# Running the middle row transform of a spectral gate's backward pass in two turns: a pair's back matmuls placed after the next pair's forward matmuls, and tiny edge copies moved to VectorE

## The chip, the cores and the metric

The kernel runs on one core of a Trainium2 chip, as one launch. The metric is the device time of that launch in microseconds (us), the median over several runs.

## The reference

The kernel computes a gated mix of two branches and all gradients of it. `x` has 2048 rows of 1024 values.

```python
def _A_ref(x, w_r, w_i):                       # spectral branch
    X = rfft2(x) * (w_r + 1j * w_i)            # w: 2048 x 513
    return irfft2(X, s=(2048, 1024))
def _B_ref(x, w1, b1, w2, b2):                 # dense branch, 1024 -> 3584 -> 1024
    r = relu(x @ w1 + b1)
    return (r * r) @ w2 + b2
g = sigmoid((x * gate_w).sum(-1))
out = g * _A_ref(A_x, ...) + (1 - g) * _B_ref(A_x, ...)
...
_out, _vjp = jax.vjp(_f, A_x, A_w_r, A_w_i, B_w1, B_b1, B_w2, B_b2, gate_w)
return (_out, *_vjp(grad_out))
```

So there are nine outputs: the mix, and the gradients of `x`, of both parts of the spectral weight, of the dense branch's four parameters, and of the gate's weight. Inputs and outputs are bfloat16.

## The kernel before

The two-dimensional transform of `x` and that of the output's gradient are made together, as matmuls with constant matrices in 16-bit floats. The 2048-point transform along the rows is split into 32 times 64 points. The dense branch's large matmuls keep TensorE busy meanwhile. In order of time:

1. `mlp_in`: the hidden layer and its gradient (`ph`, `pd`), with the first stage of the transform between its matmuls: columns and the 32-point part of the rows. The result goes to `z_scr` in memory.
2. `mlp_grads`: the gradients of the dense weights. Each of 112 turns is a group of 16 accumulating matmuls into one `pw` bank, 128x512 (L778 for the second weight, L794 for the first), emptied by a ScalarE copy `wo` (L782, L799). There are two `pw` banks, so a group can start only when the copy of the group two before it is done. Between these turns runs `spectra()`: first `fft_mid`, the middle of the row transform, which is what the change is about, then part of `fft_out`, the last stage of the transform.
3. `mlp_out`: the dense branch's output (`acc`, L866), with the rest of `fft_out` between.
4. `GradOfX.products`: the gradient of `x` (`xX`, `xV`, `xZ`, L966).

`fft_mid` handles the 32 columns of the 32x64 split in 16 mirrored pairs `m`. For each pair, before the change:

- `inputs` loads `z` (four transfers) and the rows `w` of the spectral weight (four more), for the next pair.
- `transform`: for pairs other than the first, VectorE makes `pm`, the sum and the difference of the two columns (L356, L357). Twice (n = 0, 1) two matmuls write `px` (L364), and two ScalarE copies, on 64 partitions each, put it into `x` in another order (L366). They take 2450 ns each.
- GpSimd writes the pair's edge values into `x` (L455), and it negates a row of `w` (L373).
- `products`: VectorE multiplies `x` by `w` into `t1_`, `t2_` (L377, L379) and joins them into `y` (L384, L385, twice each).
- `back`: for n = 1, 0 two matmuls write `pv` (L394). For n = 1 ScalarE copies it to `vc` (L399); for n = 0 VectorE makes `pc` from it and `vc` (L401, L402). GpSimd copies edge values of `y` into `ye` (L408 to L414), two tiny matmuls make `si` of it (L417), two tiny VectorE copies put it into `pc` (L421 to L425), and four stores from GpSimd's queue write `pc` to `y_scr` (L428).
- `grads_of_w`: VectorE makes `gs` from `x` (L434 to L438), ScalarE scales it to `gw` (L440), VectorE halves its edge values (L441), and GpSimd's queue stores it (L444).

`px` and `pv` take turns in two buffers of PSUM, two banks each (tag `ps2`). `x`, `z`, `w` and `pc` have two buffers, `pm`, `y`, `vc`, `gs` and `gw` one.

The order of the work is set by generators. `fft_mid` yields seven times for a pair. `spread` hands out `spectra()` between the turns of the gradients at a constant rate:

```python
spec, grads = spectra(), mlp_grads()
next(grads), next(grads)
todo = 1 + 7 * (R1 // 2) + 2 * NT
for _ in spread(grads, spec, todo / (2.0 * FG * FGC * NH - 2)):
    pass
```

That is 145 yields over 110 turns, about 1.32 a turn. [...]A scheduler at build time sets the order in a queue from this program order and its own idea of the durations, so a row may stand a little earlier or later than the program has it. `fft_mid` of before:

```python
for m in range(NM):
    ...
    for x in transform(m, z):
        yield
    G.tensor_copy(out=x[:, :, :, 0::H], in_=ex[:, m])
    for y in products(x, w):
        yield
    yield from back(m, y)
    grads_of_w(m, x)
    yield
```

Of the kernel before, what the change touches and what calls it, by code (L numbers as in the profile page):

```python
# [10 lines left out]
P = 128  # L11
BF16 = mybir.dt.bfloat16
FP16 = mybir.dt.float16
FP32 = mybir.dt.float32
ALU = mybir.AluOpType
ACT = mybir.ActivationFunctionType

FDT = FP16
# [117 lines left out]
def kernel(  # L136
# [22 lines left out]
    nc = tc.nc  # L159
# [6 lines left out]
    g = Geo(S, D, F)  # L166
    S2, DC, FC = g.S2, g.DC, g.FC
    R1, R2 = g.R1, g.R2
    NT = S // P
# [132 lines left out]
    def fft_mid():  # L302
# [9 lines left out]
        def inputs(m):  # L312
            z = fb.tile([P, 2, 2, H], FDT, name="z", tag="z", bufs=2)
            for n, c in enumerate((m, R1 // 2 + m)):
                for x in range(2):
                    ld(out=z[lanes[x], n], in_=z_scr[:][c, :, x ^ n if m else x])
            w = fb.tile([P, 3, LW], BF16, name="w", tag="w", bufs=2)
            for c_, src_w in enumerate((A_w_r, A_w_i)):
                for n, k in enumerate(pair_of(m, R1)):
                    ld(out=w[lanes[n], c_, 0:W1], in_=every(src_w, k))  # L320
            return z, w

        def edges():

            ed = fb.tile([P, NM, 2, 4], FDT, name="ed", tag="ed")
            low = fb.tile([P, NM, 4], FDT, name="low", tag="low")
            mid = fb.tile([P, 4], FDT, name="mid", tag="mid")
            col = z_scr[:].rearrange("c r x t l -> r c (x t) l")[:, :, :, 0]
            for e in range(4):
                ld(out=ed[lanes[0], :, 0, e], in_=col[:, 0:NM, e])  # L330
                ld(out=low[lanes[1], :, e], in_=col[:, NM:, e])
            ld(out=mid[lanes[0]], in_=col[:, NM])
            nc.vector.tensor_copy(out=ed[lanes[0], :, 1, :], in_=ed[lanes[0], :, 0, :])
            nc.vector.tensor_copy(out=ed[lanes[0], 0, 1, :], in_=mid[lanes[0]])
            for n in range(2):
                a, b = slice(2 * n, 2 * n + 2), slice(2 - 2 * n, 4 - 2 * n)
                nc.vector.tensor_copy(out=ed[lanes[1], :, n, a], in_=low[lanes[1], :, a])
                nc.vector.tensor_scalar(out=ed[lanes[1], :, n, b], in0=low[lanes[1], :, b], scalar1=-1.0, scalar2=None, op0=ALU.mult)
            nc.vector.memset(ed[lanes[1], 0], 0.0)
            sp = tps.tile([P, NM, 2, 4], FP32, name="sp", tag="tr", bufs=2)  # L340
            for m in range(NM):
                for n in range(2):
                    mm(sp[:, m, n], lhsT=am[:, m, n, :], rhs=ed[:, m, n, :], start=True, stop=True, skip_group_check=True)
            ex = fb.tile([P, NM, 2, 2, 2], FDT, name="ex", tag="ex")
            for n in range(2):
                for c in range(2):
                    nc.vector.tensor_copy(
                        out=ex[lanes[n], :, c], in_=sp[lanes[c], :, n, :].rearrange("p m (e t) -> p m t e", e=2)
                    )
            return ex  # L350

        def transform(m, z):

            if m:
                pm = fb.tile([P, 2, 2, H], FDT, name="pm", tag="pm")
                V(out=pm[:, 0], in0=z[:, 0], in1=z[:, 1], op=ALU.add)  # L356
                V(out=pm[:, 1], in0=z[:, 0], in1=z[:, 1], op=ALU.subtract)  # L357
            else:
                pm = z
            x = fb.tile([P, 2, 2, LW], FDT, name="x", tag="x", bufs=2)  # L360
            for n in range(2):
                px = fps.tile([P, 2, H], FP32, name="px", tag="ps2", bufs=2)
                for T in range(2):
                    mm(px[:, T, :], lhsT=am[:, m, n, :], rhs=pm[:, n, T, :], start=True, stop=True)  # L364
                for c in range(2):
                    nc.scalar.copy(  # L366
                        out=x[lanes[n], c, :, 0:H].rearrange("p t (i g) -> p t g i", g=4),
                        in_=px[lanes[c]].rearrange("p t (g i) -> p t g i", g=4),
                    )
                yield x  # L370

        def products(x, w):
            G.tensor_scalar(out=w[:, 2, 0:W1], in0=w[:, 1, 0:W1], scalar1=-1.0, scalar2=None, op0=ALU.mult)  # L373
            t1_ = fb.tile([P, 2, 2, LW], FDT, name="t1", tag="t1")
            t2_ = fb.tile([P, 2, 2, LW], FDT, name="t2", tag="t2")
            xw = lambda t: t[:].rearrange("p c t l -> p (c t) l")[:, :, 0:W1]
            V(out=xw(t1_), in0=xw(x), in1=w[:, 0:1, 0:W1].to_broadcast([P, 4, W1]), op=ALU.mult)  # L377
            wi = w[:, 1:3, 0:W1].rearrange("p (o t) l -> p o t l", o=1).to_broadcast([P, 2, 2, W1])
            V(out=t2_[:, :, :, 0:W1], in0=x[:, :, :, 0:W1], in1=wi, op=ALU.mult)  # L379
            yield  # L380
            y = fb.tile([P, 2, 2, LW], FDT, name="y", tag="y")
            for n in (1, 0):
                L = lanes[n]
                V(out=y[lanes[0], n, :, 0:W1], in0=t1_[L, 0, :, 0:W1], in1=t2_[L, 1, :, 0:W1], op=ALU.subtract)  # L384
                V(out=y[lanes[1], n, :, 0:W1], in0=t1_[L, 1, :, 0:W1], in1=t2_[L, 0, :, 0:W1], op=ALU.add)  # L385
            yield y

        def back(m, y):
            pc = fb.tile([P, 2, 2, H], FDT, name="pc", tag="pc", bufs=2)
            pv = {}  # L390
            for n in (1, 0):
                pv[n] = fps.tile([P, 2, H], FP32, name="pv", tag="ps2", bufs=2)
                for T in range(2):
                    mm(pv[n][:, T, :], lhsT=bm[:, m, n, :], rhs=y[:, n, T, 0:H], start=True, stop=True)  # L394
                if m == 0:
                    nc.scalar.copy(out=pc[:, n], in_=pv[n][:])
                elif n == 1:
                    vc = fb.tile([P, 2, H], FP32, name="vc", tag="vc")
                    nc.scalar.copy(out=vc[:], in_=pv[1][:])  # L399
                else:  # L400
                    V(out=pc[:, 0], in0=pv[0][:], in1=vc[:], op=ALU.add)  # L401
                    V(out=pc[:, 1], in0=pv[0][:], in1=vc[:], op=ALU.subtract)  # L402
                yield

            ye = fb.tile([P, 2, 2, 2], FDT, name="ye", tag="ye", bufs=2)
            yl = y[:, :, :, H]
            if m:
                G.tensor_copy(out=ye[:, :, 0, :], in_=yl)  # L408
                G.tensor_copy(out=ye[:, 1, 1, :], in_=yl[:, 1])
                G.tensor_scalar(out=ye[:, 0, 1, :], in0=yl[:, 0], scalar1=-1.0, scalar2=None, op0=ALU.mult)  # L410
            else:
                G.memset(ye[:], 0.0)
                for n in range(2):
                    G.tensor_copy(out=ye[:, n, n, :], in_=yl[:, n])  # L414
            sp = tps.tile([P, 2, 2], FP32, name="si", tag="tr", bufs=2)
            for n in range(2):
                mm(  # L417
                    sp[:].rearrange("p a t -> p (a t)"), lhsT=bm[:, m, n, :], rhs=ye[:, n].rearrange("p a t -> p (a t)"),
                    start=(n == 0), stop=(n == 1), skip_group_check=True,
                )  # L420
            nc.vector.tensor_copy(out=pc[lanes[1], 0, :, 0], in_=sp[lanes[0], 0, :])  # L421
            if m:
                nc.vector.tensor_copy(out=pc[lanes[0], 1, :, 0], in_=sp[lanes[1], 1, :])
            else:
                nc.vector.tensor_copy(out=pc[lanes[1], 1, :, 0], in_=sp[lanes[0], 1, :])  # L425
            for n, c in enumerate((m, R1 // 2 + m)):
                for h in range(2):
                    st(out=y_scr[:][c, :, h ^ n if m else h], in_=pc[lanes[h], n])  # L428
# [16 lines left out]

        nxt = inputs(0)
        ex = edges()
        yield
        for m in range(NM):
            z, w = nxt  # L450
            if m + 1 < NM:
                nxt = inputs(m + 1)
            for x in transform(m, z):
                yield
            G.tensor_copy(out=x[:, :, :, 0::H], in_=ex[:, m])  # L455
            for y in products(x, w):
                yield
            yield from back(m, y)
            grads_of_w(m, x)
            yield  # L460
        fbs.close()

    def fft_out():
# [680 lines left out]
    for k in range(NT // 4):  # L1144
        i = 4 * k
# [38 lines left out]
    n = 0  # L1184
# [25 lines left out]

    spec, grads = spectra(), mlp_grads()
    next(grads), next(grads)
    todo = 1 + 7 * (R1 // 2) + 2 * NT
    for _ in spread(grads, spec, todo / (2.0 * FG * FGC * NH - 2)):
        pass
    tps_s.close()
# [45 lines left out]
```

## The time and the profile before

| what | value |
|---|---|
| median time of 3 runs | 1378.58 us (1378.45 to 1379.13) |
| span of the profiled run | 1377.1 us |
| TensorE (PE) busy | 1283.7 us, 93% |
| VectorE (DVE) busy | 697.4 us, 51% |
| ScalarE (ACT) busy | 581.7 us, 42% |
| GpSimd (POOL) busy | 271.8 us, 20% |
| granted TensorE clock, mean | 0.968 |
| the four x copies of a pair (L366), all pairs | 156.8 us in 64 copies |
| negation of w on GpSimd (L373), all pairs | 24.5 us in 16 |
| GpSimd's tiny copies into `ye` and `x` (L408 to L414, L455) | 10.6 + 9.2 + 6.2 + 1.3 + 3.6 us |

A row of the profile names the line, the engine, what is written and read, and how often. PE is TensorE's matmul, PEld its load of the stationary operand, which lies beside the matmuls. In the view of waits a row says which instruction waited for which, for how long in total, how often, and the longest. In the timeline the number in brackets is the idle time of that engine just before, with what ended it. `mlp_grads` runs from 446 to about 984 us, and the 16 pairs of `fft_mid` from about 465 to 880 us. A busy TensorE is not TensorE at full speed: records of matmuls overlap, so its rate is read from the time between starts.

### The profile page before, as it was taken

What the parts mean: (1) busy time and instruction counts of PE and PEld (TensorE: products, weight loads), DVE (VectorE), ACT (ScalarE), POOL (GpSimd) and SP (SyncE); (2) the same over time, 40 slices, a digit from 0 to 9 for tenths busy, and PEclk for the clock granted to TensorE, in tenths of its full rate; (3) what the DMA queues carried; (4) which work ended last, traced back from release to release, by engine and by line L of the source; (5) the groups of instructions that cost most, each with busy time, mean ns of one, the idle gap of its engine ahead of it and who ended that gap; (6) DMA issues with size and microseconds to landing.
All of it is one profiled execution on the core that took longest, in us unless ns stands there. A gap on an engine that the chain in (4) does not pass through costs nothing.

```text
span 1377.1 us, 18208 instructions
## 1 busy us (share of the span) xinstructions
PE 1283.7 (93%) x6754; PEld 616.7 (45%) x6884; DVE 697.4 (51%) x1522; ACT 581.7 (42%) x793; POOL 271.8 (20%) x456
## 2 busy tenths in 40 slices
PE   9999999999999987987887889699999999999997
PEld 5655544555444433333333333355544445444443
DVE  4454424444822345434443543344577777795663
ACT  4656645666433465465556546244321112101110
POOL 0111111111111233432343442212100010000000
PEclk9999999999999998999899899899999999999999
DMA  9566445553437777766455665698598996845450
GB/s 294 164 181 189 140 139 167 176 171 111 128 110 172 183 177 184 191 178 151 101 146 136 145 136 117 162 319 226 168 245 187 226 228 177 229 130 168 141 150 31
DMA packets 326004, 233.27 MB, mean 169 GB/s; under 512 B 195052, under 2 KB 279178, under 8 KB 325658
## 3 DMA queue, kind: packets, MB, share of 16 engines
q1 hardware_dynamic: 290864, 141.19, 42.8%
q0 software_dynamic: 26144, 82.47, 18.0%
q10 hardware_dynamic: 8906, 8.43, 2.1%
q8 instruction: 54, 0.88, 0.3%
q14 instruction: 36, 0.29, 0.1%
HBM read 106.19 MB, written 81.81 MB: 137 GB/s over the span
## 4 chain that ended last, share of the span: by engine, by line
PE 51%; DVE 5%; ACT 4%; issue 3%; POOL 1%; DMA 1%; another core or an unknown queue 0%; POOLq 0%; ACTq 0%; DVEq 0%
PE acc L866 12%; PE pw L794 12%; PE pw L778 10%; PE xX L966 7%; PE xV L966 3%; ACT x L366 3%; PE xZ L966 2%; PE pv L394 1%; PE pki L493 1%; PE pui L294 1%; DVE t L379 1%; PE px L364 1%; DVE y L385 1%; DVE y L384 1%; DVE g L434 0%
## 5 line engine op out<-in xcount | busy, mean ns | idle before, releaser
L778 PE MATMUL pw<-dbn,grp 128*128 128x512 bf16 x876 | 214.8, 400 | 13.5 <-ACT wo L782 12.0
L637 PE MATMUL ph<-xT,w1g 128*128 128x512 bf16 x864 | 217.0, 379 | 2.7 <-DMA w1g<-in_B_w_dram 1.2
L794 PE MATMUL pw<-grp,res 128*128 128x512 bf16 x873 | 209.7, 394 | 7.8 <-ACT wo L799 6.5
L647 PE MATMUL pd<-dbT,w2T 128*128 128x512 bf16 x877 | 209.8, 379 | 1.6 <-DVE dhT L651 0.4
L866 PE MATMUL acc<-w,hblk 128*128 128x512 bf16 x873 | 196.4, 379 | 1.2
L651 DVE SCALAR_TENSOR_TENSOR dhT<-pd,rT 128x512 bf16<-128x512 f32 x112 | 77.3, 690 | 203.0 <-PE pd L647 159.8
L366 ACT CAST x<-px 64x1024 f16<-64x1024 f32 x64 | 156.8, 2450 | 3.4 <-PE px L364 2.5
L778 PEld LDWEIGHTS <-grp 128*128 128x128 bf16 x896 | 91.0, 102 | 130.0 <-issue 37.9
L794 PEld LDWEIGHTS <-res 128*128 128x128 bf16 x896 | 89.2, 101 | 115.0 <-issue 23.1
L647 PEld LDWEIGHTS <-w2T 128*128 128x128 bf16 x896 | 87.1, 98 | 103.4 <-issue 1.2
L866 PEld LDWEIGHTS <-hblk 128*128 128x128 bf16 x896 | 86.4, 98 | 98.3
L639 ACT ACTIVATE rT<-ph,b1col 128x512 bf16<-128x512 f32 x112 | 76.9, 687 | 116.1 <-PE ph L637 112.5
L637 PEld LDWEIGHTS <-w1g 128*128 128x128 bf16 x896 | 84.5, 98 | 90.5 <-DMA w1g<-in_B_w_dram 1.5
L932 ACT ACTIVATE g<-gatew_bc,dsc 128x1024 f32<-128x1024 bf16 x16 | 18.3, 1148 | 150.7 <-DVE gxo L975 124.5
L495 ACT CAST rt<-pki 128x1024 f16<-128x1024 f32 x32 | 32.5, 1017 | 97.9 <-PE pki L493 93.3
L377 DVE TENSOR_TENSOR t<-x,w 128x2052 f16<-128x2052 f16 x16 | 19.7, 1232 | 106.1 <-POOL x L455 106.0
L640 ACT ACTIVATE h2T<-rT 128x512 bf16<-128x512 bf16 x112 | 70.6, 630 | 2.5
L799 ACT CAST wo<-pw 128x512 bf16<-128x512 f32 x56 | 32.2, 585 | 92.6 <-PE pw L794 51.5
L966 PEld LDWEIGHTS <-dS 128*128 128x128 f16 x448 | 43.8, 98 | 52.9
L394 PE MATMUL pv<-y,bm 128*128 128x512 f16 x64 | 23.1, 455 | 45.9 <-DVE y L385 45.8
L782 ACT CAST wo<-pw 128x512 bf16<-128x512 f32 x56 | 31.8, 586 | 64.1 <-PE pw L778 42.2
L283 POOL DMA_DIRECT2D z_scr<-u x32 | 22.8, 714 | 171.5 <-ACT u L278 101.6
(186 smaller groups left out, 1581.9 us busy)
## 6 DMA issues: line engine op xcount, KB each, us to landing
h2T_scr<-h2T POOLq DMA_DIRECT2D x28, 512.0 KB, 4.3
dhT_scr<-dhT POOLq DMA_DIRECT2D x28, 512.0 KB, 4.7
hblk<-h2T_scr SPq DMA_DIRECT2D x8, 1792.0 KB, 9.2
hblk<-dhT_scr SPq DMA_DIRECT2D x8, 1792.0 KB, 8.8
z_scr<-u POOLq DMA_DIRECT2D x32, 256.0 KB, 3.1
z<-z_scr SPq DMA_DIRECT2D x64, 128.0 KB, 3.2
y_scr<-pc POOLq DMA_DIRECT2D x64, 128.0 KB, 2.8
r<-y_scr ACTq DMA_DIRECT2D x32, 256.0 KB, 4.3
```

The costliest lines, as they stand in the source:

```text
L366: nc.scalar.copy(out=x[lanes[n], c, :, 0:H].rearrange("p t (i g) -> p t g i", g=4), in_=px[lanes[c]].rearrange("p t (g i) -> p t g i", g=4),)
L394: mm(pv[n][:, T, :], lhsT=bm[:, m, n, :], rhs=y[:, n, T, 0:H], start=True, stop=True)
L495: nc.scalar.copy(out=rt[n][:], in_=pk[:])
L637: mm(ph[:], lhsT=w1g[:, dc, fc % 2 * P : (fc % 2 + 1) * P], rhs=xT[:, dc, ss], start=(dc == 0), stop=(dc == DC - 1))
L639: nc.scalar.activation(rT[:], ph[:], ACT.Relu, bias=b1col[:, fc : fc + 1])
L640: nc.scalar.activation(h2T, rT[:], ACT.Square)
L647: mm(pd[:], lhsT=w_[:, ec, fc % FGC * P : (fc % FGC + 1) * P], rhs=dbT[:, ec, ss], start=(ec == 0), stop=(ec == DC - 1),)
L651: return STT(out=dhT, in0=pd[:], scalar=2.0, in1=rT[:], op0=ALU.mult, op1=ALU.mult, accum_out=gb1part[:, fc, sb : sb + 1],)
L778: mm(pw[:], lhsT=cur[:, t, fb_ * P : (fb_ + 1) * P], rhs=dbn[:, t, hf * H : (hf + 1) * H], start=(t == 0), stop=(t == NT - 1),)
L794: mm(pw[:], lhsT=xr[t][:, d_ * P : (d_ + 1) * P], rhs=cur[:, t, :], start=(t == 0), stop=(t == NT - 1),)
L866: turn["PE"] = mm(acc[:], lhsT=cur[:, fc, t2 * P : (t2 + 1) * P], rhs=w2[:, fc, cs], start=(fc == 0), stop=(fc == FC - 1))
L966: mm(acc[:], lhsT=lhs[:, fc, :], rhs=rhs[:, fc, :], start=start and fc == 0, stop=fc == KH - 1, skip_group_check=True,)
```

## The change

`fft_mid` works on two pairs in turn. The forward matmuls of pair m come first; after them come the back matmuls of pair m-1, whose `y` was joined in the turn before. The purpose is that TensorE should not stand waiting for the VectorE products of the very pair whose forward matmuls it has just made. A pair's `y` and `ye` are held over to the next turn (`held`). The inputs are loaded a turn earlier, and `pm` has two buffers. A turn now has six yields, and the constant that sets the rate is changed with it.

Second, the tiny copies and the negation that GpSimd did (`w`, `ye`, the edges of `x`) run on VectorE. Nothing that is computed changes.

```diff
-        def transform(m, z):
+        def mirrored(m, z):
...
+            pm = fb.tile([P, 2, 2, H], FDT, name="pm", tag="pm", bufs=2)
...
         def products(x, w):
-            G.tensor_scalar(out=w[:, 2, 0:W1], in0=w[:, 1, 0:W1], scalar1=-1.0, scalar2=None, op0=ALU.mult)
+            nc.vector.tensor_scalar(out=w[:, 2, 0:W1], in0=w[:, 1, 0:W1], scalar1=-1.0, scalar2=None, op0=ALU.mult)
...
-                G.tensor_copy(out=ye[:, :, 0, :], in_=yl)
+                nc.vector.tensor_copy(out=ye[:, :, 0, :], in_=yl)
...
+        pm, w = mirrored(0, nxt[0]), nxt[1]
+        nxt = inputs(1)
+        held = None
         yield
-        for m in range(NM):
-            z, w = nxt
-            if m + 1 < NM:
-                nxt = inputs(m + 1)
-            for x in transform(m, z):
-                yield
-            G.tensor_copy(out=x[:, :, :, 0::H], in_=ex[:, m])
-            for y in products(x, w):
-                yield
-            yield from back(m, y)
-            grads_of_w(m, x)
-            yield
+        for m in range(NM + 1):
+            if m < NM:
+                x = fb.tile([P, 2, 2, LW], FDT, name="x", tag="x", bufs=2)
+                for n in range(2):
+                    transform(m, n, pm, x)
+                    yield
+                nc.vector.tensor_copy(out=x[:, :, :, 0::H], in_=ex[:, m])
+            if held:
+                backs = back(m - 1, *held)
+                next(backs)
+                yield
+            if m < NM:
+                ts = products(x, w)
+            if held:
+                next(backs)
+                yield
+                for _ in backs:
+                    pass
+            if m < NM:
+                held = joined(m, *ts)
+                yield
+                grads_of_w(m, x)
+                if m + 1 < NM:
+                    pm, w = mirrored(m + 1, nxt[0]), nxt[1]
+                if m + 2 < NM:
+                    nxt = inputs(m + 2)
+                yield
...
-    todo = 1 + 7 * (R1 // 2) + 2 * NT
+    todo = 1 + 6 * (R1 // 2) + 2 * NT
```

In the new code `products` ends with `t1_` and `t2_`, the join into `y` and the copies into `ye` are a function of their own (`joined`), and `back` gets both.

More of the change, by code (lines that the diff above doesn't have):

```diff
@@ L350, in edges, with transform @@
             return ex
-        def transform(m, z):
[L354 to L370, printed above, removed]
+        def mirrored(m, z):
+            if m == 0:
+                return z
+            pm = fb.tile([P, 2, 2, H], FDT, name="pm", tag="pm", bufs=2)
+            V(out=pm[:, 0], in0=z[:, 0], in1=z[:, 1], op=ALU.add)
+            V(out=pm[:, 1], in0=z[:, 0], in1=z[:, 1], op=ALU.subtract)
+            return pm
+        def transform(m, n, pm, x):
+            px = fps.tile([P, 2, H], FP32, name="px", tag="ps2", bufs=2)
+            for T in range(2):
+                mm(px[:, T, :], lhsT=am[:, m, n, :], rhs=pm[:, n, T, :], start=True, stop=True)
+            for c in range(2):
+                nc.scalar.copy(
+                    out=x[lanes[n], c, :, 0:H].rearrange("p t (i g) -> p t g i", g=4),
+                    in_=px[lanes[c]].rearrange("p t (g i) -> p t g i", g=4),
+                )
         def products(x, w):
-            G.tensor_scalar(out=w[:, 2, 0:W1], in0=w[:, 1, 0:W1], scalar1=-1.0, scalar2=None, op0=ALU.mult)
+            nc.vector.tensor_scalar(out=w[:, 2, 0:W1], in0=w[:, 1, 0:W1], scalar1=-1.0, scalar2=None, op0=ALU.mult)
             t1_ = fb.tile([P, 2, 2, LW], FDT, name="t1", tag="t1")
@@ L379, in products, with joined @@
             V(out=t2_[:, :, :, 0:W1], in0=x[:, :, :, 0:W1], in1=wi, op=ALU.mult)
-            yield
+            return t1_, t2_
+        def joined(m, t1_, t2_):
             y = fb.tile([P, 2, 2, LW], FDT, name="y", tag="y")
@@ L385, in products @@
                 V(out=y[lanes[1], n, :, 0:W1], in0=t1_[L, 1, :, 0:W1], in1=t2_[L, 0, :, 0:W1], op=ALU.add)
[L386 to L402, printed above, removed]
-                yield
             ye = fb.tile([P, 2, 2, 2], FDT, name="ye", tag="ye", bufs=2)
@@ L407, in back @@
             if m:
-                G.tensor_copy(out=ye[:, :, 0, :], in_=yl)
-                G.tensor_copy(out=ye[:, 1, 1, :], in_=yl[:, 1])
-                G.tensor_scalar(out=ye[:, 0, 1, :], in0=yl[:, 0], scalar1=-1.0, scalar2=None, op0=ALU.mult)
+                nc.vector.tensor_copy(out=ye[:, :, 0, :], in_=yl)
+                nc.vector.tensor_copy(out=ye[:, 1, 1, :], in_=yl[:, 1])
+                nc.vector.tensor_scalar(out=ye[:, 0, 1, :], in0=yl[:, 0], scalar1=-1.0, scalar2=None, op0=ALU.mult)
             else:
-                G.memset(ye[:], 0.0)
+                nc.vector.memset(ye[:], 0.0)
                 for n in range(2):
-                    G.tensor_copy(out=ye[:, n, n, :], in_=yl[:, n])
+                    nc.vector.tensor_copy(out=ye[:, n, n, :], in_=yl[:, n])
+            return y, ye
+        def back(m, y, ye):
+            pc = fb.tile([P, 2, 2, H], FDT, name="pc", tag="pc", bufs=2)
+            for n in (1, 0):
+                pv = fps.tile([P, 2, H], FP32, name="pv", tag="ps2", bufs=2)
+                for T in range(2):
+                    mm(pv[:, T, :], lhsT=bm[:, m, n, :], rhs=y[:, n, T, 0:H], start=True, stop=True)
+                if m == 0:
+                    nc.scalar.copy(out=pc[:, n], in_=pv[:])
+                elif n == 1:
+                    vc = fb.tile([P, 2, H], FP32, name="vc", tag="vc")
+                    nc.scalar.copy(out=vc[:], in_=pv[:])
+                else:
+                    V(out=pc[:, 0], in0=pv[:], in1=vc[:], op=ALU.add)
+                    V(out=pc[:, 1], in0=pv[:], in1=vc[:], op=ALU.subtract)
+                yield
             sp = tps.tile([P, 2, 2], FP32, name="si", tag="tr", bufs=2)
```

## The prediction

> **What bounds the kernel now.** I read four views in this order: the page's busy slices, TensorE's waits in the stage that the change touches, that stage's timeline, and the same stage's busy times.
>
> ```profile
> PE   9999999999999987987887889699999999999997
> PEclk9999999999999998999899899899999999999999
> ```
>
> TensorE is full except in slices 15 to 25, at 34.4 us each: about 515 to 895 us. That is where the middle row transform (`fft_mid`) runs between the matmuls of the weight gradients (`mlp_grads`). Everything else is at 90% or more, so the whole effect must come from this stretch.
>
> ```profile
> engine line waited for: us in total, times, longest us
> PE pv L394 <- DVE y L385: 45.8, 10, 4.6
> PE pw L778 <- ACT wo L782: 12.0, 5, 3.3
> PE pw L794 <- ACT wo L799: 6.5, 2, 3.3
> PE pki L493 <- DMA r<-y_scr: 6.5, 1, 6.5
> ```
>
> TensorE's waits from 446 to 985 us add up to 71 us. The largest by far is the one that the change is about: the back matmuls `pv` wait for the products `y` of their own pair.
>
> ```profile
> 618.43 4.91 ACT L366 CAST x<-px 64x1024 f16<-64x1024 f32 x2
> 623.71 1.23 DVE L377 TENSOR_TENSOR t<-x,w 128x2052 f16<-128x2052 f16 x1 [5.75 <-POOL x L455]
> 628.17 1.04 PE L394 MATMUL pv<-y,bm 128*128 128x512 f16 x2 [4.64 <-DVE y L385]
> 629.00 4.66 PE L778 MATMUL pw<-dbn,grp 128*128 128x512 bf16 x16
> ```
>
> The chain of one pair: ScalarE's two copies of `px` end at 623.3, VectorE multiplies and joins until 628.2, and only then may TensorE, idle for 4.64 us, run `pv`. After the idle time it is also slow: from 628.17 to the next `pv` at 633.50 are 5.33 us, where 2 + 16 matmuls take 0.43 + 3.45 = 3.88 elsewhere ("16 in 3.45" stands all over the chain of waits).
>
> ```profile
> 446.00:985.00 539.00, 465.05 (x2199) 211.94 (x2242) 227.46 (x448) 282.93 (x256) 179.63 (x310) 0.93 0.66 169
> ```
>
> (Columns: window, length, busy PE, PEld, DVE, ACT, POOL, clock, DMA share, GB/s.) The loss in this stage: its 112 groups of 16 `pw` at 3.45 us are 386.4; 128 matmuls of `px` and `pv` at 0.216 are 27.6; row and column matmuls of `fft_out` (16 x 0.44 + 15 x 0.52 from the timeline) 14.8; the small ones about 2. Sum 431 of 539 us, so 108 us are lost: 71 in waits, about 37 in slow matmuls after 16 waits longer than 2.5 us (2.3 us each).
>
> How long may a wait be before matmuls slow down? Two lines bracket it:
>
> ```profile
> 471.02 6.42 PE L778 MATMUL pw<-dbn,grp 128*128 128x512 bf16 x28 [1.14 <-ACT wo L782]
> 1203.24 4.88 PE L966 MATMUL xX<-w1Tr,hblk 128*128 128x512 bf16 x14 [2.71 <-DVE dT L961]
> ```
>
> After 1.14 us 28 recorded matmuls take 6.42 us: full rate. After 2.71 us 14 take 4.88 where 3.02 is usual: 1.9 us lost.
>
> **What the Trainium skill says.** "TensorE: Matmul & The Clock Gate", Part 1, has the clock halve after an idle window of about 3.4 us and return after about 3.4 us of work, with a window that runs freely. The trace agrees on the halving, but already shows it after 2.71 us; I use the trace's bracket. The same page (engine queue depths, under the array's architecture) calls ScalarE's and VectorE's queues strictly first-in first-out: a ready copy stands behind one that waits. The trace agrees: at 677 us `wo` comes only after four `x` copies, and TensorE waits 3.24 us for it. "VectorE: DVE Perf Modes", perf-mode table, lets a 16-bit `tensor_scalar` in SBUF run up to four elements a cycle; the price follows below.
>
> **The change part by part.** I use the order in which the instructions of both built programs stand on each engine.
>
> *1. The wait of `pv` for `y` goes.* In the new order `pv` of pair m-1 follows `px` of pair m; its `y` is then 20 us old. Removed: all ten waits, 45.8 us, and their slow stretches (10 x 2.3 = 23).
>
> *2. A pair has six turns for seven, so about 5 `pw` groups instead of 5.3.* In the regular pair TensorE's order is px0, group A, px1, B, pv1, C, pv0, D, si, E. At full speed: 5 x 3.45 + 8 x 0.216 + 0.1 = 19.1 us, against 400/16 = 25 now.
>
> *3. New waits through ScalarE.* Its queue in nine of the pairs (3 to 7, 12 to 15) reads x0 x0, wo(A), x1 x1, wo(B), vc, gw, wo(C), wo(D), wo(E). From px0 at time 0 with durations of the trace: x copies start at 0.72 and end at 5.63; wo(A); the second copies run from 6.28 to 11.19. pv1 (ready at 7.76) finds its bank free since 5.63; pv0 (ready at 11.64) since 11.19: no wait. But `gw` needs `gs`, and VectorE gets there only after the edge copy, two products (2.28), `g1`, `g2` and two `gs` (2.0): 11.19 + 4.65 = 15.84. `gw` takes 1.06, wo(C) behind it ends at 17.4. Group E needs the bank that wo(C) empties; TensorE is ready at 15.65. Wait 1.8 us, pair 20.9 us. Queued behind `gw` are wo(C), wo(D); both are waited for only by TensorE. Nine pairs: 16 us.
>
> *4. Pairs off the pattern.* Pairs 2, 10, 11 have pv1 and pv0 next to each other: pv0 then stands ready at 8.2 and waits for the second copies at 11.2, 3.0 us, plus a slow stretch of 2, plus about 1.5 because their `gw` comes after the whole join and holds wo(D). 6.5 each, 19.5 together. Pair 8 (px0 and px1 together) and pair 9 (px1 and pv1 together) give 2.7 and 4.3. At the start the two `px` of pair 1 have one `pw` between them, and both `pv` of pair 0 wait for 9.8 us of copies with about 5 us of work to cover them: 5 lost plus two slow stretches, 9.
>
> *5. Small operations from GpSimd to VectorE.* The negated row of w took 1.53 us on GpSimd. On VectorE it is bounded by the scaling of `kg` (128x256, 283 ns) and of `dbn` (128x1024, 480 ns); the skill's price 58 + FD/Accel cycles at 0.96 GHz gives an estimate of 0.19 to 0.33. I take 0.35. The edge copies cost 0.16 as `pc` from `si` does (159 ns); four of them, so 1.0 us a pair, 16 us for all. Of it only the edge copy into x (0.2) lies on the chain of step 3, replacing 0.2 on GpSimd. The rest is hidden: VectorE works 12.7 us in a pair of 21. The new wait: the negation waits for the load of w, with `pm` and the next pair's products behind it on VectorE. GpSimd waited 15.5 us in all for these loads. The negation stands about 8 us ahead of the next x copies' end, so I count 0, at most 15.5.
>
> *6. Start of `fft_out`.* Now 6.5 us of waiting plus slow matmuls: the last edge column is 16 us ahead of its first use. In the new order 31 `pw` (6.7 us) cover: edge copies 0.4, issue 1 to 2, landing 4.9, load 4.3. I take a wait of 4.5 and 2 slow.
>
> *7. The rest* (start of the stage, later stalls) stays: 5.
>
> Sum of losses: 16 + 19.5 + 7 + 9 + 6.5 + 5 = 63. To this the clock after the nine waits of 1.8 us, between the two bracketing lines: 0 if such a wait is harmless, 9 x 2.1 = 19 if each is punished. With a window that runs freely I expect four of nine: 8. Together 71. Gain 108 - 71 = 37 us: 1378.6 - 37 = 1341.6, say 1341.
>
> **The rivals.**
> - *TensorE becomes the bound, no new waits* (chance 0.10). For it: step 3 misses by only 1.8 us, ScalarE needs 14.8 of 19.1 us. Against: `gw` stands ahead of wo(C) in nine pairs. Then nearly all is won: losses of 5 for the rest, 6.5 at `fft_out`, 9 at the start, 5 for pairs off the pattern: 25. Time 1378.6 - 83 = 1296.
> - *Half clock after every residual wait* (0.17). For it: 2.71 us suffices to slow matmuls. Against: 1.14 does not. All nine are punished (11 more than I took) and a few us come late: 1341 + 11 + 3 = 1355.
> - *A wait in place of the one removed, slower* (0.05). VectorE's queue blocks on the loads of w and the products come late in every pair, so that each pair loses what it loses now (108 us in all), and the 16 us of moved work come on top: 1378.6 + 16 = 1394. Against: 8 us of slack; the loads already come early enough for GpSimd.
>
> **How the numbers follow.** The forecast of step by step waits has 0.68 (about 1322 to 1350), the full gain 0.10, half clock 0.17, slower 0.05. The likeliest gives 1341. The range takes in half clock with its late loads (1359) and a forecast without the 1.8 us waits: 1341 - 16 - 8 = 1317. Faster by over 0.2%: all but the last, less 0.01 for a tie: 0.94; within 0.2% 0.01; slower 0.05.
>
> **What would show it.** Right: TensorE's wait of `pv` for `y` is gone; in its place some 15 to 30 us on ScalarE's `wo` and about 10 to 15 on ScalarE's `x` copies; the stage from the first `pw` to the first `acc` takes about 502 us; the POOL row falls by some 55 us (24.5 + 10.6 + 9.2 + 6.2 + 3.6 + 1.3) and the DVE row rises by about 16; ACT stays at 582. Step 3 is wrong if `wo` doesn't hold group E for 1.5 to 2 us; step 4 if `pv` behind `pv` doesn't wait. The forecast fails if VectorE's negation waits for its load while `y` or `pm` is awaited, or if more than 12 waits of TensorE exceed 2.5 us.

## The result, and the profile after

| | us, median | range | ratio to before |
|---|---|---|---|
| before | 1378.53 | 1378.45 to 1379.13 | |
| after | 1324.74 | 1323.51 to 1326.70 | 0.961, interval 0.9594 to 0.9627 |

The change saves 53.8 us, 3.9%. The forecast was 1341, with a range from 1317 to 1359. Its mechanism holds and its gain (37 us) was a third too small.

Busy slices of the page after, for TensorE and its granted clock:

```profile
PE 1259.8 (95%) x6753; PEld 612.4 (46%) x6884; DVE 703.5 (53%) x1602; ACT 580.0 (44%) x793; POOL 215.8 (16%) x376
...
PE   9999999999999979999889988999999999899997
...
PEclk9999999999999999999999999999999999999999
```

The dent between slices 15 and 25 is nearly gone, and the clock's row is full. The first line splits the gain. Before, the profiled span was 1377.1 with TensorE busy for 1283.7: idle 93.4. Now it is 1323.3 less 1259.8: idle 63.5. So 29.9 us came from waits and 23.9 us from the same matmuls running faster, as far as the modelled ends of the records let the two be told apart.

TensorE's waits from 440 to 940 us after the change (in total, how often, the longest):

```profile
PE pv L404 <- ACT x L366: 19.2, 9, 3.0
PE pw L796 <- ACT wo L800: 10.0, 8, 1.6
PE pw L812 <- ACT wo L817: 6.3, 4, 1.6
PE pki L511 <- DMA r<-y_scr: 4.2, 2, 3.3
```

The wait of `pv` for `y` (45.8 us in ten) no longer exists. Two others stand in its place, both on ScalarE, as the forecast said: `pv` on the copies of `px`, and `pw` on the copy `wo` that stands behind `gw`. Together they are 35.5 us.

A regular pair in the timeline after; in brackets is the engine's idle time just before, and what ended it:

```profile
603.86 1.06 ACT L440 ACTIVATE gw<-gs 128x1026 bf16<-128x1026 f16 x1 [3.01 <-DVE gs L438]
604.82 1.05 ACT L800 CAST wo<-pw 128x512 bf16<-128x512 f32 x2
605.44 3.61 PE L796 MATMUL pw<-dbn,grp 128*128 128x512 bf16 x16 [1.54 <-ACT wo L800]
...
626.23 7.07 PE L796 MATMUL pw<-dbn,grp 128*128 128x512 bf16 x31 [1.60 <-ACT wo L800]
```

ScalarE waits 3 us for `gs`, then does `gw`, and only then the `wo` that empties the bank of the next group. TensorE loses 1.54 us to it. From one such wait to the next are 20.8 us; the forecast was 20.9.

The stage and three short windows of it after (window, length, busy PE, PEld, DVE, ACT, POOL, clock, DMA share, GB/s):

```profile
446.00:931.00 485.00, 441.88 (x2192) 207.31 (x2235) 232.81 (x524) 280.01 (x253) 122.68 (x228) 0.98 0.74 187
489.63:493.63 4.00, 4.00 (x12) 1.55 (x12) 3.94 (x6) 2.39 (x3) 1.06 (x2) 0.60 0.92 221
605.44:609.44 4.00, 4.00 (x19) 1.85 (x19) 3.92 (x5) 0.74 (x2) 1.88 (x4) 1.00 0.44 124
712.23:716.23 4.00, 4.00 (x11) 1.47 (x11) 3.90 (x6) 1.48 (x2) 0.54 (x1) 0.57 0.19 64
```

The stage took 539 us and takes 485: 54 us, the whole gain. The three windows begin where TensorE starts again after a wait of 3.02, 1.54 and 2.80 us. After these two long waits the clock is at 0.60 and 0.57 and 11 or 12 matmuls fit into 4 us; after the short one it is at 1.00, and 19 fit. A long wait doesn't always do it: behind one of 2.99 us, just before the first window, the clock stayed at 1.00. All nine waits of 1.54 to 1.60 us left it at 1.00, which is the largest single reason why the gain became larger than forecast.

### The profile page after: what moved, and what is told of

The parts are those of the page before. It is cut to its first block, busy times and chain, and to the rows that moved or that the text cites. A ratio compares the mean times of both kernels' runs of the same rounds, so it can differ in the third digit from the quotient of the medians.

```text
span 1323.3 us, 18166 instructions
## 1 busy us (share of the span) xinstructions
PE 1259.8 (95%) x6753; PEld 612.4 (46%) x6884; DVE 703.5 (53%) x1602; ACT 580.0 (44%) x793; POOL 215.8 (16%) x376
## 3 DMA queue, kind: packets, MB, share of 16 engines
q0 software_dynamic: 26144, 82.47, 18.5%
## 5 line engine op out<-in xcount | busy, mean ns | idle before, releaser
L796 PE MATMUL pw<-dbn,grp 128*128 128x512 bf16 x876 | 204.4, 385 | 11.1 <-ACT wo L800 10.0
L812 PE MATMUL pw<-grp,res 128*128 128x512 bf16 x872 | 202.4, 383 | 7.6 <-ACT wo L817 6.3
L366 ACT CAST x<-px 64x1024 f16<-64x1024 f32 x64 | 156.8, 2451 | 3.2 <-PE px L364 2.5
L796 PEld LDWEIGHTS <-grp 128*128 128x128 bf16 x896 | 88.2, 99 | 118.4 <-issue 18.8
L884 PEld LDWEIGHTS <-hblk 128*128 128x128 bf16 x896 | 86.5, 98 | 98.2
L513 ACT CAST rt<-pki 128x1024 f16<-128x1024 f32 x32 | 32.4, 1014 | 102.3 <-PE pki L511 94.0
L984 PEld LDWEIGHTS <-hblk 128*128 128x128 bf16 x336 | 32.7, 98 | 43.9 <-DMA hblk<-dhT_scr 3.7
L984 PE MATMUL xX<-dT,dS 128*128 128x512 f16 x224 | 51.0, 379 | 0.0
```

Source lines behind the costliest of these rows:

```text
L366: nc.scalar.copy(out=x[lanes[n], c, :, 0:H].rearrange("p t (i g) -> p t g i", g=4), in_=px[lanes[c]].rearrange("p t (g i) -> p t g i", g=4),)
L513: nc.scalar.copy(out=rt[n][:], in_=pk[:])
L796: mm(pw[:], lhsT=cur[:, t, fb_ * P : (fb_ + 1) * P], rhs=dbn[:, t, hf * H : (hf + 1) * H], start=(t == 0), stop=(t == NT - 1),)
L812: mm(pw[:], lhsT=xr[t][:, d_ * P : (d_ + 1) * P], rhs=cur[:, t, :], start=(t == 0), stop=(t == NT - 1),)
L884: turn["PE"] = mm(acc[:], lhsT=cur[:, fc, t2 * P : (t2 + 1) * P], rhs=w2[:, fc, cs], start=(fc == 0), stop=(fc == FC - 1))
L984: mm(acc[:], lhsT=lhs[:, fc, :], rhs=rhs[:, fc, :], start=start and fc == 0, stop=fc == KH - 1, skip_group_check=True,)
```

## The experiments

Theory A is that of the forecast: the gain comes from the order of matmuls in two turns, the moved small operations are hidden, what is left is `gw` ahead of `wo` on ScalarE and `pv` behind `pv`, and a wait costs extra only when it is long enough to lower the clock. Its rivals: the freed GpSimd or the second `pm` buffer carries the gain; every wait that is left is punished by the clock; the turns win because they take a wait out, but a shorter chain would have done so as well.

**Turns alone (turns_only) and small operations alone (copies_only).**

```diff
 # turns_only, on the kernel after; and likewise ye and the edges of x
-            nc.vector.tensor_scalar(out=w[:, 2, 0:W1], in0=w[:, 1, 0:W1], scalar1=-1.0, scalar2=None, op0=ALU.mult)
+            G.tensor_scalar(out=w[:, 2, 0:W1], in0=w[:, 1, 0:W1], scalar1=-1.0, scalar2=None, op0=ALU.mult)
 # copies_only, on the kernel before; and likewise ye and the edges of x
-            G.tensor_scalar(out=w[:, 2, 0:W1], in0=w[:, 1, 0:W1], scalar1=-1.0, scalar2=None, op0=ALU.mult)
+            nc.vector.tensor_scalar(out=w[:, 2, 0:W1], in0=w[:, 1, 0:W1], scalar1=-1.0, scalar2=None, op0=ALU.mult)
```

> The two turns as in the change, but the tiny copies and the negation of w stay on GpSimd. Theory (the order of the turns carries the gain, the moved copies nothing): 1325 us, within 3 of the changed kernel; no wait of pv for y, the nine waits of about 1.57 us on wo again. Rival (the move to VectorE carries part of the gain, since GpSimd's queue holds the edge copy into x and the copies into ye in front of stores): 1335 to 1350 us, with VectorE waiting on GpSimd's x and si on GpSimd's ye.

> The kernel before with only the tiny copies and the negation of w on VectorE. Theory: 1378 us, within 3 of before; ten waits of pv for y of about 4.6 us remain, GpSimd loses 55 us of busy time for nothing. Rival (the move carries part of the gain): 1360 us or less, with waits of pv shorter by the hops over GpSimd. Third possibility (VectorE's extra 16 us and the negation's wait for its load lie ahead of y): 1385 to 1394 us.

Measured: turns_only 1328.52 us, 0.9631 (0.9615 to 0.9646); copies_only 1375.89, 0.9979 (0.997 to 0.9987). The turns carry about 50 of the 54 us, the small operations 3 to 4 either way, which is no more than two runs of one kernel differ here (copies_only: 1373.4 to 1378.5), though for copies_only, with 16 runs, the interval excludes 1. With the small operations on GpSimd the nine waits on `wo` are 1.66 to 2.01 us long instead of 1.54 to 1.60, and a tenth, of 1.93 us, ends at 649 us. With them on VectorE in the kernel before, `pv` still waits for `y` 44.1 us, and VectorE's negation waits 35.2 us for its load (11.9 of it before the first pair) without harm to the time.

**One buffer for pm (pm_one).**

```diff
-            pm = fb.tile([P, 2, 2, H], FDT, name="pm", tag="pm", bufs=2)
+            pm = fb.tile([P, 2, 2, H], FDT, name="pm", tag="pm")
```

> The changed kernel with one buffer for pm, as before. Theory: pm stands a pair ahead in VectorE's queue and with one buffer it is made after px of the pair before, some 13 us before its use; 1325 us, within 3. Rival (the second buffer keeps px from waiting for pm): waits of px on pm, 1330 us or more.

Measured: 1323.64 us, 0.9603 (0.9583 to 0.9623). The second buffer carries nothing that can be seen in the time.

**gw off ScalarE's queue (gw_vector), and twice in it (gw_twice).** In gw_twice the same values are written a second time; nothing is left out.

```diff
 # gw_vector
-            nc.scalar.mul(out=gw[:, :, 0:W1], in_=gs[:, :, 0:W1], mul=GS)
+            nc.vector.tensor_scalar(out=gw[:, :, 0:W1], in0=gs[:, :, 0:W1], scalar1=GS, scalar2=None, op0=ALU.mult)
 # gw_twice
             nc.scalar.mul(out=gw[:, :, 0:W1], in_=gs[:, :, 0:W1], mul=GS)
+            nc.scalar.mul(out=gw[:, :, 0:W1], in_=gs[:, :, 0:W1], mul=GS)
```

> The changed kernel with gw scaled on VectorE, so that no ScalarE copy stands behind the wait for gs. Theory (the wait of group E is set by gw ahead of wo in ScalarE's queue): the nine waits of about 1.57 us go, 14 us, so 1310 us; pv still waits for x copies about 19 us. Rival (ScalarE is loaded so densely that the next row of its queue takes over, or the longer VectorE queue delays pc): waits reappear elsewhere, 1318 to 1326 us.

> The changed kernel with the scaling of gw on ScalarE written twice (the second writes the same values again), which lengthens the nine waits of 1.57 us by about 1.0 to about 2.6 us. Theory A (a wait of some 2 us and more halves the clock for the matmuls behind it): 9.5 us of longer waits plus 9 x 1.9, so about 1350 us, and 16 matmuls after such a wait take about 5 us. Theory B (short waits are harmless as long as TensorE has been busy around them): only the longer waits, about 1334 us, 16 matmuls in 3.6 us.

Measured: gw_vector 1311.05 us, 0.9506 (0.9492 to 0.9521): the nine waits are gone, and the time falls by about their sum (13.7 us for 14.1). gw_twice 1353.53, 0.9823 (0.9803 to 0.9843): with one more microsecond in each of the nine waits the time rises by 28.8 us. Between the two profiled runs TensorE's idle time grows by 16.6 us (63.5 to 80.1), of which the nine waits are 10.0, and its busy time by 11.4 (1259.8 to 1271.2), which is slower matmuls. The windows after four of these waits in gw_twice, of 2.62, 2.62, 2.62 and 2.99 us (columns as above), say why:

```profile
567.24:571.24 4.00, 4.00 (x11) 1.50 (x11) 3.21 (x10) 0.44 (x1) 2.61 (x5) 0.57 1.17 282
614.23:618.23 4.00, 4.00 (x12) 1.55 (x12) 3.40 (x11) 0.44 (x1) 1.45 (x3) 0.63 0.32 101
637.73:641.73 4.00, 4.00 (x19) 1.85 (x19) 3.38 (x11) 0.79 (x2) 3.12 (x6) 1.00 1.19 279
545.44:549.44 4.00, 4.00 (x19) 1.85 (x19) 3.27 (x9) 0.79 (x2) 3.31 (x7) 1.00 0.73 253
```

Waits of equal length lower the clock or leave it. The wait's length alone doesn't decide, but in this kernel it sets the odds: at 1.6 us the clock falls behind none of the nine, at 2.6 to 3.0 us behind seven.

**Half of the px copies on VectorE, by partitions (x_split, x_split_gw, before_x_split).** The second is x_split with the edit of gw_vector; the third is the kernel before with this edit alone.

```diff
             for c in range(2):
-                nc.scalar.copy(
+                (nc.vector.tensor_copy if c else nc.scalar.copy)(
```

> The changed kernel with the second of each two x copies on VectorE instead of ScalarE. VectorE's copy is estimated at 1.2 us, from pc out of PSUM (128x1024 f32, 1224 ns). Theory (what is left of the loss are ScalarE's four x copies of 2.45 us, which delay wo, vc, gw and hold the banks that pv needs): the second copies end about 4 us earlier, the nine waits on wo and nearly all of the 19 us of pv on x copies go, about 1293 us. Rival (VectorE, which already works 12.7 us a pair, becomes the late one: its copies stand behind the join of the pair before): pv waits on VectorE's x copies, 1315 us or more.

> As x_split, with gw scaled on VectorE too. Theory: no more than 2 us below x_split, since gw is no longer waited for once x comes early; about 1292 us. Rival (VectorE is the late one): slower than x_split by up to 8 us.

> The kernel before, with nothing but the second of each two x copies on VectorE: the pair's chain is cut instead of being held over to the next turn. Theory: the ten waits of pv for y shrink from 4.6 to about 0.6 to 1.0 us, because px's copies end 4 us earlier; the 18.5 us of waits on wo go too, and with the long waits the slow matmuls; 6.5 us for r stay. About 1295 us, so faster than the change. Rival (the dependence of pv on its own pair's y keeps costing, since the products alone need some 5 us and VectorE gets more work): waits of 2 us and more remain, 1330 us or more.

Measured: x_split 1304.36 us, 0.946 (0.9445 to 0.9476); x_split_gw 1300.82, 0.9435 (0.9415 to 0.9454); before_x_split 1356.59, 0.9832 (0.9815 to 0.9848). Each is faster than the kernel on which it splits the copies (after, gw_vector and before), and all three miss their forecast: by 11, 9 and 62 us. Between x_split and x_split_gw the ranges overlap. Two assumptions were wrong. VectorE's copy takes 2.46 us, not the 1.2 estimated from `pc`; and I had taken it that the two halves run side by side. They don't. The two engines in the timeline of x_split_gw:

```profile
602.53 2.46 ACT L366 CAST x<-px 64x1024 f16<-64x1024 f32 x1
...
605.02 2.47 DVE L366 CAST x<-px 64x1024 f16<-64x1024 f32 x1 [1.19 <-ACT x L366]
```

VectorE is ready, but starts when ScalarE ends (602.53 + 2.46 = 604.99). So the split only unloaded ScalarE; the chain from `px` to `x` stayed 4.9 us long. In before_x_split the wait of `pv` for `y` is still 44.8 us in 19 waits, and what went are the 18.5 us on `wo`.

**By bank (bank_split_gw, before_bank_split), and with two tiles (two_px_gw, before_two_px).** The kernels named gw have the edit of gw_vector as well.

```diff
 # both: T=0 to ScalarE, T=1 to VectorE, two copies each
-            for c in range(2):
-                nc.scalar.copy(
-                    out=x[lanes[n], c, :, 0:H].rearrange("p t (i g) -> p t g i", g=4),
-                    in_=px[lanes[c]].rearrange("p t (g i) -> p t g i", g=4),
-                )
+            for T in range(2):
+                for c in range(2):
+                    (nc.vector.tensor_copy if T else nc.scalar.copy)(
+                        out=x[lanes[n], c, T, 0:H].rearrange("p (i g) -> p g i", g=4),
+                        in_=px[lanes[c], T].rearrange("p (g i) -> p g i", g=4),
+                    )
 # the two_px kernels also
-            px = fps.tile([P, 2, H], FP32, name="px", tag="ps2", bufs=2)
+            px = [fps.tile([P, H], FP32, name="px", tag="ps2", bufs=2) for T in range(2)]
```

> After the change, gw on VectorE, and px copied out by bank: ScalarE takes T=0, VectorE T=1, two copies of 512 elements each (before: halves of 64 partitions over both banks, where VectorE's half started only when ScalarE's had ended, 602.53 + 2.46 = 604.99 and then 605.02). Theory A (two engines that read the same banks of px are put one after the other, so the split by partitions only unloaded ScalarE and left the chain of 4.9 us): by bank the copies run side by side, a px is out in about 2.6 us, the wait of pv for x (13.3 us in 7 waits) falls to under 6, and the time is about 1290 us (1286 to 1296). Rival B (the copies are still put in turn, or four short copies cost more than two long ones): pv for x stays above 10 us and the time at 1298 us or more.

> The kernel before, in one turn, with px copied out by bank: ScalarE T=0, VectorE T=1. The wait of pv for y was 4.6 us ten times; with the split by partitions it was still 3.1 us ten times, because the two halves ran one after the other. Theory A (in one turn the wait is the length of the chain px, copies, products, y; shorten the chain by 2.3 us a px and the wait falls by as much): pv for y about 0.8 us ten times, matmuls behind it at full rate, 1315 to 1330 us, so that the shorter chain does without turns nearly what the turns do. Rival B (the chain's end is held by something else, the edge copy on GpSimd or VectorE's queue): waits stay above 2.5 us and the time at 1345 us or more.

> As bank_split_gw, but px is two tiles of one bank each, T=0 for ScalarE and T=1 for VectorE, out of the same four banks' slots (two slots: one px takes both). In bank_split_gw VectorE's copy still began only at the end of ScalarE's (14.7 us of pv for x in 8 waits). Theory A (what puts the copies in turn is the shared tile px): they now run side by side, pv waits for x no more than 4 us in all. A new wait then comes in its place: px of the second half needs VectorE's copy of the first to be out, and VectorE is in the join of the pair before until about 2.9 us after the first px; it ends 5.5 us after it, where the second px is ready after 3.9 us: 1.6 us in about ten pairs, 16 us, so the time stays at 1298 to 1306 us. Rival B (VectorE is early enough): the waits are gone and the time is 1284 to 1294 us. Rival C (the tile isn't the cause): pv for x stays above 10 us.

> The kernel before, in one turn, with px as two tiles, one copied out by ScalarE and one by VectorE. In before_bank_split the two still took turns (613.07 to 615.70 behind 610.41 to 613.03), pv waited 3.5 us for y ten times, and the time was 1363. Theory A (in one turn the wait is the length of the chain px, copies, products, y): side by side the copies end 2.6 us earlier, the ten waits fall from 3.5 to about 0.9 us, matmuls behind them run at full rate, and the time is 1310 to 1330 us, near what the turns reach. Rival B (something else than the copies ends the chain): ten waits above 2.5 us and 1350 us or more.

Measured: bank_split_gw 1303.07 us, 0.9447 (0.9432 to 0.9462); before_bank_split 1363.09, 0.9883 (0.9867 to 0.99); two_px_gw 1298.44, 0.9405 (0.9385 to 0.9424); before_two_px 1307.26, 0.9476 (0.9461 to 0.9491).

Split by bank the copies still take turns, as in the timeline of bank_split_gw:

```profile
666.92 2.62 ACT L367 CAST x<-px 64x512 f16<-64x512 f32 x2
...
669.58 2.63 DVE L367 CAST x<-px 64x512 f16<-64x512 f32 x2 [3.09 <-ACT x L367]
```

So both kernels land where their rival B put them, before_bank_split because of this order and not for the reason that its rival gave. The Trainium skill, "PSUM — Partial Sum Buffer", section on bank collisions, forbids two engines on the same bank and the same 32 partitions at once, reads included; neither split has that, so the page asked for no order here. What orders them is the shared tile `px`: in bank_split_gw VectorE's copies wait 38.4 us for ScalarE's, in 26 waits, and with two tiles of one bank each no such wait is left and the copies start together. (The two tiles also lie in two different slots of `ps2`; that this matters wasn't tried by itself.) The timeline of two_px_gw:

```profile
603.16 2.63 DVE L367 CAST x<-px 64x512 f16<-64x512 f32 x2
603.17 2.63 ACT L367 CAST x<-px 64x512 f16<-64x512 f32 x2
```

The same in the kernel before, with one turn (before_two_px), its waits from 440 to 940 us and the windows after two of them, a wait of 1.50 us for `x` and one of 1.55 us for `y`:

```profile
PE pv L395 <- DVE y L386: 11.5, 11, 1.5
PE px L364 <- ACT x L367: 8.9, 6, 1.5
PE pki L494 <- DMA r<-y_scr: 7.7, 1, 7.7
```

```profile
551.63:555.63 4.00, 4.00 (x19) 1.85 (x19) 3.30 (x3) 3.19 (x3) 0.59 (x2) 1.00 1.09 290
536.96:540.96 4.00, 4.00 (x19) 1.86 (x20) 3.84 (x7) 2.07 (x2) 3.23 (x5) 1.00 0.56 156
```

The wait for `y` isn't removed, only cut from 4.6 to at most 1.55 us, and no matmul behind it is slow any more: from 470 to 810 us the mean clock is 1.00. The kernel is 71.3 us below before, more than the change's 53.8; 55.8 of it came with the two tiles, from before_bank_split's 1363.1, whose one turn, engines and copies are the same. So the last rival stands: the turns are one of two ways to the same gain. They hide the chain of a pair behind another pair; the two tiles shorten it until its waits no longer lower the clock. The two gains don't add up: on top of the turns the two tiles bring 4.6 us (1303.1 to 1298.4). Both together have the lowest median, though x_split_gw, in turns without the two tiles, has 1300.8 with an overlapping range. The new wait that I expected there, `px` behind VectorE's copy of the half before, is 1.4 us in all, not 16, and `pv` waits 6.5 us for `x`, not at most 4 (theory A of that run was wrong in both); waits of `px` and `pv` on the copies are 12.2 us in all.

## Why the prediction was right, and where it was off

1. *The wait of `pv` for `y` goes.* Right: none is left, and its slow stretches went with it. From the wait to the next `pv`, as in the prediction's example, the ten of them measure 1.3 to 2.9 us, 21 in all, for the 23 taken.
2. *Six turns, about five `pw` groups a pair.* Right; the period was 20.8 us for the 20.9 of step 3.
3. *Nine pairs wait for `wo` behind `gw`.* Right in number, place and cause: the nine are at pairs 3 to 7 and 12 to 15, 1.54 to 1.60 us each, 14.1 us for my 16. gw_vector shows the cause.
4. *Pairs off the pattern.* Right in kind, too dear. Pairs 2, 10 and 11 wait 2.80, 2.88 and 2.80 us and then run slow: 2 + 16 matmuls take 5.57, 5.43 and 5.57 us where 3.88 is usual, 4.9 us in all. But `wo(D)` behind their `gw` cost 0.50 us once, not 1.5 each: 13.9 us for my 19.5. Pairs 8 and 9 gave 2.1 and 2.6 us for 2.7 and 4.3. The start gave 6.0 us of waits and one slow stretch of 1.5, 7.5 for 9.
5. *Small operations.* Right that they are hidden: copies_only and turns_only differ from their counterparts by 3 and 4 us, both in favour of VectorE. POOL fell by 56.0 us (forecast 55). The added operations take 15.5 us on VectorE in their own records (forecast 16), yet its row rose by only 6.1; part is that the edge of `gw` became shorter (317 to 178 ns), and part that short records overlap the one before: its groups' own times add up to 12.2 us more (776.7 to 788.9). The negation took 294 ns, inside the estimate of 0.19 to 0.33 us, and the edge copies 171 to 184 ns. VectorE's negation waited 9.5 us for its loads and delayed nothing that I could find.
6. *Start of `fft_out`.* Waits of 3.30 and 0.90 us for my 4.5; the slow stretch behind it is about 2.8 us for 2 (from 825.80 to 833.86 are 7.2 us without the second wait, where 16 `pki` at 57 ns and 16 `pw` make 4.4).
7. *The rest.* What the terms above leave of the stage's loss, 485 - 431 = 54 us: 6.8 for my 5.

The sum was 71 and is 54. Most of the 17 us between them are two terms: the clock after the nine waits, where I put 8 us between 0 and 19 and the trace shows 0 (the clock is at 1.00 behind every one of them), and the 5.6 us of step 4. The first was a guess: in the trace before TensorE has no wait between 1.21 and 2.71 us, so nothing there could decide it. Of the signs named, the waits on `wo` (16.3 us) fall in their range; those on `x` (19.2) exceed theirs, the stage took 485 us and not 502, and six waits of the stage, not more than 12, exceed 2.5 us.

Two figures of the prediction don't follow from its own lines: the old period, 400/16 = 25 us, is 415/16 = 26 from the bounds of 465 and 880 us, and the upper end of the range, 1359, lies 4 us above the 1355 that its rival adds up to. The likeliest time rests on neither.

The rival "half clock after every residual wait" is refuted at 1.6 us, but gw_twice shows that it wasn't far off: one microsecond more, and the clock falls behind seven of the nine. (That gw_twice took 1353.5 us, near the rival's 1355, is chance: it holds longer waits that the rival doesn't count.) The rival of full gain, 1296, is refuted for this kernel, which keeps 35.5 us of waits on ScalarE. The slower one is refuted by the same load waits that it rested on: they happened, and were hidden.

What stays open is where the 3 us of the small operations come from. Shorter `wo` waits can't be all of it: in the kernel before these waits are 18.5 us with and without the move, while the wait of `pv` for `y` fell from 45.8 to 44.1 us. After the change `xX` in the last stage waits 3.2 us for `hblk`, where before it waited 2.7 us for `dT`. This is no new wait: `xX` waits once for 2.6 to 3.8 us in every one of the fourteen traces, and what differs is which of `hblk`, `dT` and `dg` comes last.

## What to carry to other kernels

Sum TensorE's waits, but weigh them by length: here a wait of `pv`, `px` or `pw` below 2 us cost itself, and the ten of 4.2 to 4.7 us cost themselves and about half as much again in slow matmuls (45.8 and 21 us), so cutting a long wait to a short one also wins the slow matmuls behind it. Before pipelining a chain over two turns, see whether two links of it run one after the other without need: two engines that empty one tile were put in turn, and giving each a tile of its own (55.8 us in the kernel before) was worth as much as the two turns (53.8), and little once the turns were there (4.6). When a change moves waits to another engine, read that engine's queue in order: the next gain was one instruction that waits (`gw`) ahead of one that is waited for (`wo`).

## What the runs showed of the hardware that I had not expected

*When the clock falls.* Over the 14 traces I took every wait of `pv`, `px` and `pw` above 1.2 us in this stage and the granted clock of the 4 us after it.

```
wait, us        waits   clock 0.50 to 0.69   clock 1.00
1.21 to 1.93       62                    0           62
2.01 to 3.06       48                   37           11
3.09 to 4.65       53                   53            0
```

The Trainium skill, "TensorE: Matmul & The Clock Gate", Part 1, gives an idle window of about 3.4 us that runs freely. The runs agree that the length alone doesn't decide, for the middle row holds both outcomes at equal length, but the shortest wait of the table with a lowered clock behind it is far shorter than 3.4 us: 2.03 us, in before_x_split, with this window behind it.

```profile
671.29:675.29 4.00, 4.00 (x12) 1.55 (x13) 2.83 (x6) 1.20 (x2) 2.19 (x4) 0.62 0.87 201
```

The table isn't a safe limit. It leaves out the waits of `sp` (tiny matmuls that make the edge values at the start of `fft_mid`) and of `pki` (matmuls of `fft_out`), and there shorter ones have a lowered clock behind them: one of `sp` of 1.69 us in before_x_split, with 32 tiny matmuls of 128x4 in the first 1.4 us after it, and four of `pki` of 1.42 to 1.86 us, each of which ends 3 to 4 us after another wait of 2.8 to 3.1 us. The window behind the one of `sp`:

```profile
468.83:472.83 4.00, 4.00 (x43) 2.10 (x43) 2.32 (x7) 0.59 (x1) 1.16 (x3) 0.75 0.63 145
```

In three of the eleven cases with 1.00 in the middle row a second long wait takes up more than half of the 4 us. What else than the length decides isn't shown by these runs.

*ScalarE and VectorE empty `px` at the same speed.* A copy of 64x1024 from PSUM with the elements reordered on the way out took 2451 ns on ScalarE and 2464 ns on VectorE, against 1014 ns for ScalarE's copy of 128x1024 out of `pki`. So VectorE was no faster engine to move it to, and what shortened it here was running both at once. Whether the new order of the elements is what makes the copy slow wasn't tried.
